# V with two keys per partition and copied-up odd keys, and expert weights as the moving operand in four column groups

## The chip, the core and the metric

The kernel runs on one core of one Trainium2 chip. The metric is device time in microseconds (us) of one execution. Several executions are made of each kernel, on the same chip as executions of the kernel before; medians are quoted with the lowest and highest run. A profiled execution gives the lines shown below. PE is the matrix engine (TensorE), PEld its weight loads, DVE is VectorE, ACT is ScalarE, POOL is GpSimd, SP is the engine that here only issues DMAs; a name with a q behind it (SPq, ACTq) is the engine's issuing of work. L243 is line 243 of that kernel. "Clock" is the mean share of full speed that was granted to PE.

Ratios are computed as the mean time of one kernel's fast runs over the mean time of the kernel before's fast runs in the same rounds, with a 95% interval. They are therefore not quite the ratio of the medians that are quoted. A run counts as fast when it is within 1.5% of the fastest run of its kernel, so a ratio can rest on few runs.

## The reference, cut to what matters

The computation is attention with "beacon" keys that every query may see, followed by a mixture of experts with soft slots.

```python
B, H, S, Nb, D = 8, 8, 576, 16, 64          # batches, heads, tokens, beacons, head size
k_all = concat([beacon_k, k], axis=2)       # 592 keys per head, beacons first
v_all = concat([beacon_v, v], axis=2)
scores = q @ k_all.T / sqrt(D)              # beacons always seen, the rest causal
a = exp(scores - max); a /= a.sum(-1)
x = (a @ v_all) -> reshaped to [4608, 512]

logits = x @ phi                            # [4608, 32]: 8 experts x 4 slots
slot_input = softmax(logits, axis=0).T @ x  # [32, 512]
for e in range(8):                          # w1 [512,1024], w2 [1024,512] per expert, float32
    slot_out[e] = relu(slot_input[e] @ w1[e]) @ w2[e]
out = softmax(logits, axis=1) @ slot_out    # [4608, 512]
```

## The kernel before

The loop goes over 32 pairs of heads, four pairs (g = 0 to 3) to a batch. In each step PE computes the scores of pair n in four pieces, ACT takes their exponential, POOL zeroes the entries above the diagonal, and PE multiplies the exponentials of pair n-1 with V. Work of the previous batch's routing is spread between. q and k are loaded five pairs ahead. V of the next batch is loaded in four parts, one per pair, and cast from float32 to float16 into `vh`, one key per partition.

```python
def load_v(b, part):
    for c in ((0, 1), (2,), (3,), (4,))[part]:          # c: block of 128 keys
        vf[(b, c)] = vfp.tile([P, H, D], FP, ...)
        if c == 0:
            nc.sync.dma_start(out=vf[(b, c)][0:Nb], in_=beacon_v[b].rearrange("h n d -> n h d"))
        lo, hi = max(0, c * P - Nb), min(S, (c + 1) * P - Nb)
        p0 = lo + Nb - c * P
        nc.sync.dma_start(out=vf[(b, c)][p0:p0 + hi - lo],
                          in_=v[b, :, lo:hi, :].rearrange("h p d -> p h d"))

def cast_v(b, c):
    (nc.vector if c % 2 else nc.gpsimd).tensor_copy(out=vh[b % 2][0:kn, c, :, 0:D], in_=vf[(b, c)][0:kn])

# in score(n, 0): one mask for the four diagonal blocks of both heads, on POOL
nc.gpsimd.affine_select(out=ex[n][:, :, 0:512]..., compare_op=AL.is_ge, fill=0.0, ...)

for n in range(NP + 1):
    ...                                                  # score, transp(n + 1), attend(n - 1)
    if n + 5 < NP:
        load_pair(n + 5)                                 # q and k
    if b + 1 < B:
        load_v(b + 1, g)
        for c in ((), (0, 1), (2,), (3, 4))[g]:
            cast_v(b + 1, c)
    if n % 3 != 2 and n >= 3 and wl < 24:
        load_w(wl); wl += 1                              # expert weights, 0.5 MB a piece, on POOL's queue

for e in range(E):                                       # experts: weights are the stationary operand
    for t in range(NFC):
        for c in range(NDC):
            nc.tensor.matmul(hp[:, t, :], w1h[e][:, c * F + t * P:c * F + (t + 1) * P],
                             siT[:, c, e * SPE:(e + 1) * SPE], ...)
    nc.scalar.activation(hTz[:, e, :, e * SPE:(e + 1) * SPE], hp[:, :, :], AF.Relu)
    for t in range(NFC):
        nc.tensor.matmul(sop[0:NSL, :], hTz[:, e, t, :], w2h[e][:, t * Dm:(t + 1) * Dm], ...)
```

The softmax here doesn't subtract the row's maximum and nothing guards it: scores larger than these inputs give would overflow.

## Time and profile before

The kernel before took 239.38 us (237.88 to 241.59, 3 runs); its profiled execution spans 239.4 us.

| what | before |
|---|---|
| attention with routing | to 181.5 us |
| experts | 181.5 to 211.2 us |
| output | 211.2 to 239.4 us |
| POOL idle until a V load landed | 28.5 us in 12 waits |
| steps of a batch that nothing disturbs | 3.45 + 3 x 4.76 = 17.7 us |
| steps of a batch as measured (starts of the key transposes) | 18.7 to 21.8 us |

The first fence is the view by windows of the kernel before: the window, its length, busy time of each engine with instruction counts, then the granted PE clock, the DMA engines' busy share and the GB/s moved.

```profile
core 0: us, PE busy (x) PEld busy (x) DVE busy (x) ACT busy (x) POOL busy (x), PEclk, DMA share, GB/s
0.00:24.00 24.00, 13.88 (x249) 10.61 (x249) 12.51 (x27) 9.83 (x11) 8.31 (x20) 1.00 1.05 249
24.00:181.50 157.50, 131.79 (x2911) 100.53 (x2910) 103.88 (x256) 104.16 (x150) 75.33 (x134) 0.92 0.99 220
181.50:211.20 29.70, 27.37 (x321) 13.70 (x321) 0.57 (x2) 1.58 (x8) 5.78 (x8) 0.77 1.06 186
211.20:239.40 28.20, 14.08 (x36) 4.25 (x35) 13.87 (x19) 11.83 (x18) 0.00 (x0) 0.58 0.81 335
```

The reader should see that in the attention no engine is busy for more than 84% of the window, while the DMA engines' share is 0.99. (The share is the sum of the packets' times over 16 engines, so it can exceed 1.)

The second fence is the view of POOL's waits, kernel before: what waited, for what, us in total, how often, the longest.

```profile
POOL vh_138 L243 <- DMA vf<-in_v_dram: 19.0, 7, 5.8
POOL vh_137 L243 <- DMA vf<-in_v_dram: 9.5, 5, 4.3
```

These two lines are the 28.5 us: POOL stands before a V cast because V has not landed, and the masks behind it in POOL's queue are late.

The third fence holds two of the costliest groups, kernel before (busy us, mean ns of one, then idle before it), and the fourth two DMA issues (KB each, median us from issue to landing).

```profile
L210 POOL TENSOR_SCALAR_AFFINE_SELECT ex<-ex 128x1024 f16<-128x1024 f16 x32 | 34.9, 1092 | 46.9 <-ACT ex L208 46.9
L243 POOL CAST vh_138<-vf 128x512 f16<-128x512 f32 (+1 forms) x12 | 7.7, 639 | 19.0 <-DMA vf<-in_v_dram 19.0
```

```profile
qf<-in_q_dram SPq DMA_DIRECT2D x32, 288.0 KB, 6.2
vf<-in_v_dram SPq DMA_DIRECT2D x24, 256.0 KB, 7.0
```

The trace also records every DMA packet with its size and duration. V moves in 37888 packets of 256 bytes, at 18 ns in the median (1024 packets of beacon keys have the same size and stay in all counts and sums for V here, 38912 packets in total); q and k in 8192 packets of 2304 bytes at 93 ns. The times of all packets of a kind, added up and divided by 16 engines, are called "packet time": V 54.0 us, q and k 56.0 us.

### The profile page before, as it was taken

How to read it: one execution, taken by the hardware profiler on the slowest of the kernel's cores; microseconds unless marked ns; L12 is line 12 of the kernel's file. 1: busy time of each engine (PE TensorE's matmuls, PEld its weight loads, DVE VectorE, ACT ScalarE, POOL GpSimd, SP SyncE). 2: the span in 40 equal slices, each digit the busy share in tenths (PEclk: the TensorE clock that was granted, in tenths of full speed). 3: DMA queues.
4: the chain of work that ended last, by engine and by line, in shares of the span. 5: the costliest groups of instructions: out<-in, count | busy, mean ns of one | idle time of the engine just before them, and what ended most of it. 6: DMA issues, size and time to landing. Idle time of an engine off the chain costs nothing.

```text
span 239.4 us, 8048 instructions
## 1 busy us (share of the span) xinstructions
PE 187.1 (78%) x3512; PEld 129.1 (54%) x3512; DVE 130.8 (55%) x304; ACT 127.4 (53%) x187; POOL 89.4 (37%) x161
## 2 busy tenths in 40 slices
PE   0579778869986898797898698899869999979800
PEld 0457566647664766575666476677646445532200
DVE  4583967555777566777667666566652000058800
ACT  2075576747767487776786758477710000057700
POOL 4080645442652732744645363443542420000000
PEclk9999889985999799999999979689996569995555
DMA  6999999999899899999999999272599999919995
GB/s 193 225 300 281 317 225 243 298 258 240 220 248 228 193 230 282 205 273 263 258 317 262 230 201 277 43 127 41 92 161 202 209 206 210 159 81 422 416 413 248
DMA packets 63715, 55.63 MB, mean 232 GB/s; under 512 B 41920, under 2 KB 50112, under 8 KB 62656
## 3 DMA queue, kind: packets, MB, share of 16 engines
q1 hardware_dynamic: 50880, 38.35, 56.3%
q0 software_dynamic: 12800, 16.78, 41.5%
q8 instruction: 27, 0.44, 0.8%
q14 instruction: 8, 0.07, 0.1%
HBM read 62.46 MB, written 9.44 MB: 300 GB/s over the span
## 4 chain that ended last, share of the span: by engine, by line
PE 47%; DMA 16%; ACT 13%; DVE 5%; SPq 5%; POOL 5%; issue 4%; ACTq 0%
DMA vf<-in_v_dram 14%; ACT ex L208 10%; PE av_152 L397 8%; PE sc_156 L202 6%; PE av_152 L229 6%; PE tr L187 6%; PE fp L413 5%; PE tr L256 3%; DVE xT L261 3%; PE tr L392 3%; PE sc_157 L202 3%; SPq L103 3%; PE tr L271 2%; PE av_153 L229 2%; DMA kf<-in_k_dram 2%
## 5 line engine op out<-in xcount | busy, mean ns | idle before, releaser
L208 ACT ACTIVATE ex<-sc_156 128x1024 f16<-128x1024 f32 x64 | 63.0, 984 | 47.4 <-PE sc_156 L202 47.2
L208 ACT ACTIVATE ex<-sc_157 128x992 f16<-128x992 f32 x64 | 48.0, 751 | 12.2 <-PE sc_157 L202 12.1
L210 POOL TENSOR_SCALAR_AFFINE_SELECT ex<-ex 128x1024 f16<-128x1024 f16 x32 | 34.9, 1092 | 46.9 <-ACT ex L208 46.9
L229 PEld LDWEIGHTS <-ex 128*128 128x128 f16 (+2 forms) x960 | 40.6, 113 | 12.8 <-issue 10.9
L397 PE MATMUL av_152<-w2h,hTz 128*32 128x512 f16 x64 | 20.1, 471 | 2.3 <-ACT hTz L395 2.3
L187 PE MATMUL tr<-idb,kf 64*64 64x64 bf16 x576 | 16.6, 204 | 2.0 <-issue 0.8
L261 DVE COPY xT<-tr 128x1024 f16<-128x1024 f16 x16 | 10.5, 687 | 13.2 <-PE tr L256 13.2
L187 PEld LDWEIGHTS <-qf 64*64 64x64 bf16 x576 | 13.4, 118 | 7.4 <-issue 6.2
L187 PE MATMUL tr<-idb,qf 64*64 64x64 bf16 x576 | 16.8, 205 | 0.6 <-DMA qf<-in_q_dram 0.5
L395 ACT ACTIVATE hTz<-tr 128x32 f16<-128x32 f32 x8 | 1.6, 198 | 28.8 <-PE tr L392 28.8
L401 DVE TENSOR_SCALAR soh<-av_152,rd 32x512 f16<-32x512 f32 x1 | 0.7, 737 | 29.0 <-PE av_152 L397 29.0
L187 PEld LDWEIGHTS <-kf 64*64 64x64 bf16 x576 | 14.3, 119 | 2.9 <-issue 2.6
L413 PE MATMUL fp<-soh,eLh 32*128 32x512 f16 x36 | 14.1, 522 | 1.4 <-DVE soh L401 0.8
L415 ACT ACTIVATE osb<-fp,rc 128x512 f32<-128x512 f32 x18 | 11.8, 687 | 5.9 <-PE fp L413 5.6
L202 PE MATMUL sc_156<-qT_129,kT_132 64*128 64x128 bf16 (+1 forms) x110 | 9.6, 276 | 6.9 <-POOL kT_132 L192 4.8
L243 POOL CAST vh_138<-vf 128x512 f16<-128x512 f32 (+1 forms) x12 | 7.7, 639 | 19.0 <-DMA vf<-in_v_dram 19.0
L216 POOL TENSOR_SCALAR_AFFINE_SELECT ex<-ex 80x160 f16<-80x160 f16 x32 | 10.6, 331 | 10.7 <-ACT ex L208 10.3
L202 PEld LDWEIGHTS <-kT_132 64*128 64x128 bf16 (+1 forms) x198 | 8.6, 110 | 11.1 <-POOL kT_132 L192 5.7
L417 DVE TENSOR_SCALAR osb<-fp,rc 128x512 f32<-128x512 f32 x18 | 13.1, 748 | 2.4 <-PE fp L413 1.6
L120 POOL DMA_DIRECT2D w1h<-in_moe_w_dram x16 | 11.5, 724 | 6.6 <-PE tr L392 6.6
L120 POOL DMA_DIRECT2D w2h<-in_moe_w_dram x16 | 12.1, 758 | 4.4 <-PE av_152 L397 4.4
L229 PE MATMUL av_153<-vh_138,ex 128*128 128x65 f16 (+2 forms) x240 | 11.5, 202 | 2.1 <-issue 2.1
(206 smaller groups left out, 318.9 us busy)
## 6 DMA issues: line engine op xcount, KB each, us to landing
qf<-in_q_dram SPq DMA_DIRECT2D x32, 288.0 KB, 6.2
kf<-in_k_dram SPq DMA_DIRECT2D x32, 288.0 KB, 6.3
w1h<-in_moe_w_dram POOLq DMA_DIRECT2D x16, 512.0 KB, 8.6
w2h<-in_moe_w_dram POOLq DMA_DIRECT2D x16, 512.0 KB, 8.9
out_dram<-osb SPq DMA_DIRECT2D x8, 1024.0 KB, 8.2
vf<-in_v_dram SPq DMA_DIRECT2D x24, 256.0 KB, 7.0
vf<-in_v_dram SPq DMA_DIRECT2D x8, 224.0 KB, 6.9
vf<-in_v_dram SPq DMA_DIRECT2D x8, 160.0 KB, 7.2
```

Source lines behind the costliest of these rows:

```text
L120: nc.gpsimd.dma_start(out=d[e][:, o:o + 2048].rearrange("p (c f) -> p c f", c=c), in_=src)
L187: nc.tensor.transpose(tp[po:po + 64, j, :], hi, idb[po:po + 64, po:po + 64])
L202: nc.tensor.matmul(sc[0:kn, a, col:col + un], kT[n % 3][64 * a:64 * a + 64, P * c:P * c + kn], qT[n % 3][64 * a:64 * a + 64, u0:u0 + un], ...
L208: nc.scalar.activation(ex[n][:, :, o:o + w], sc[:, :, 0:w], AF.Exp, scale=scale)
L210: nc.gpsimd.affine_select(out=ex[n][:, :, 0:512].rearrange("p a (c t) -> p a c t", c=4), in_=ex[n][:, :, 0:512].rearrange("p a (c t) -> p ...
L216: nc.gpsimd.affine_select(out=ex[n][0:UL, :, o:o + UL], in_=ex[n][0:UL, :, o:o + UL], compare_op=AL.is_ge, fill=0.0, base=0, pattern=[[0, ...
L229: nc.tensor.matmul(avs[a][0:m, i * DD:(i + 1) * DD], ex[n][0:kn, a, o:o + m], vh[b % 2][0:kn, c, h, :], start=(c == 0), stop=(c == i))
L261: nc.vector.tensor_copy(out=xT[b][:, :, P * cs[0]:P * cs[0] + 2 * P].rearrange("p t (i u) -> p i t u", i=2), in_=tp[:, :, :, :])
L397: nc.tensor.matmul(sop[0:NSL, :], hTz[:, e, t, :], w2h[e][:, t * Dm:(t + 1) * Dm], start=(e == 0 and t == 0), stop=(e == E - 1 and t == NF ...
L413: nc.tensor.matmul(fp_[:, :], etok(cg, j), soh[:, :], start=True, stop=True)
L415: nc.scalar.activation(osb[:, j, :], fp_[:, :], AF.Copy, scale=rc[:, i:i + 1])
L417: nc.vector.tensor_scalar(out=osb[:, j, :], in0=fp_[:, :], scalar1=rc[:, i:i + 1], scalar2=None, op0=AL.mult)
```

## The change

The intent is to move V in packets of twice the size and to shorten PE's work in the experts. A pair of neighbouring keys is put in one partition, so that a packet is 512 bytes. Blocks of scores below the diagonal then take even and odd keys separately, with rows chosen by a stride of 2. The blocks on the diagonal need keys in such an order that a 128-query block sees only 128 keys: for them a second copy `vn` is made, whose lower 64 partitions are the even keys and whose upper 64 the odd ones. POOL copies the even half, and a DMA from tile to tile (the "lift") moves the odd half up. The diagonal mask becomes a multiply on DVE with a fixed 0/1 tile; the triangular masks of the blocks beside the diagonal stay on POOL. In the experts the weights become the moving operand (512 columns), with the 32 slots as the stationary operand in four column groups.

```diff
 def load_v(b, part):
+    if part == 2:                                  # last 80 keys, one per partition, 256 B packets
+        nc.sync.dma_start(out=t[0:UL, :, :], in_=v[b, :, 4 * P - Nb:S, :].rearrange("h p d -> p h d"))
+    else:
+        t = vfp.tile([P, H, 2 * D], FP, name="vf", tag="vf")
+        vr = v[b].rearrange("h (r e) d -> r h (e d)", e=2)
+        if part == 0:
+            nc.sync.dma_start(out=t[0:Nb // 2, :, :], in_=beacon_v[b]...)          # partitions 0 to 7
+            nc.sync.dma_start(out=t[Nb // 2:P, :, :], in_=vr[0:P - Nb // 2, :, :]) # partitions 8 to 127
+        else:
+            nc.sync.dma_start(out=t[:, :, :], in_=vr[P - Nb // 2:2 * P - Nb // 2, :, :])
 ...
+        elif st == 3:                              # in score(): the blocks on the diagonal
+            z = ex[n][:, soff[3]:EW]
+            nc.vector.tensor_tensor(out=z, in0=z, in1=own..., op=AL.mult)
 ...
 def cast_v(b, part):
+    for e in range(2):
+        nc.gpsimd.tensor_copy(out=w[:, 2 * part + e, :, 0:D], in_=vf[(b, part)][:, :, e * D:(e + 1) * D])
+    nc.gpsimd.tensor_copy(out=vn[b % 2][0:64, part, :, :], in_=w[0:64, 2 * part, :, :])
+
+def lift_v(b):
+    for C in range(2):
+        nc.sync.dma_start(out=vn[b % 2][64:P, C, :, :], in_=vh[b % 2][0:64, 2 * C + 1, :, :])
 ...
             if b + 1 < B:
-                load_v(b + 1, g)
-                for c in ((), (0, 1), (2,), (3, 4))[g]:
-                    cast_v(b + 1, c)
+                for part in ((0, 1), (2,), (), ())[g]:
+                    load_v(b + 1, part)
+                if g > 0:
+                    cast_v(b + 1, g - 1)
+                if g == 2:
+                    lift_v(b + 1)
 ...
+def layer1(e):                                     # experts: weights move, 512 columns at a time
+    for f in range(2):
+        for c in range(NDC):
+            nc.tensor.matmul(sc[NSL * c:NSL * (c + 1), f, :], siT[:, c, :],
+                             w1h[e][:, c * F + f * 512:c * F + (f + 1) * 512], ...)
+    # copies to hs; turn(e) adds the four groups and transposes by a 0/1 "pick" matrix; layer2(e) alike
```

## The prediction

> What bounds the kernel now. The chain of waits has three stages: attention with routing until about 181 us, experts 181.5 to 211.2, output 211.2 to 239.4.
>
> Attention. Undisturbed, four pairs take about 17.7 us (3.45 + 3 x 4.75, starts of the key transposes in the timeline); measured batches take 19.3 to 21.8. The waits view names the cause: POOL sits 28.5 us before the V casts of line 243, waiting for V's loads; the masks and the kT copy queue behind, and PE stalls for 1.5 to 2.7 us (34.6, 75.9, 97.5, 135.7 us; also 25.3). Some of these stalls drop the granted clock to 0.5 (28, 79, 137 us). Together 12 to 13 us. A further 2.1 us gap at 50 us ("issue") with its slow clock is not V's. The DMA is also nearly full here (share 1.0 to 1.2 until 150 us): per batch, median packet times sum to about 19.2 us, of which V takes 5.3 (4736 packets of 256 B at 18 ns, 14 B/ns; the 2304 B packets of q and k reach 25 B/ns).
>
> Experts. PE is 90% busy, but the weight DMA runs without a gap from 174 to 209 us, 2.54 us per 0.5 MB piece; the last piece lands about 2 us before the experts end. So this stage is already almost DMA-bound.
>
> Output: DMA-bound at 420 GB/s.
>
> What the change does.
> 1. V goes in 512 B packets. [...] (18 ns at 256 B, 93 at 2304, 313 at 8192). My estimate is 28 to 31 ns at 512 B: V falls from 5.3 to about 4.3 us per batch, 8 us over the kernel.
> 2. V is loaded at least one pair before its cast; before, the last part was loaded and cast in the same pair. This should end POOL's V wait.
> 3. Masks: the 1092 ns one is gone; one of 512 and two of 256 columns come (estimated 630 and 405 ns from 290 ns at 128 and 1092 at 1024), plus a DVE multiply [...]. All casts move to POOL with two copies. POOL rises from 89 to about 120 us; in two of four pairs it does about 4.5 us of work in 4.75. That is thin.
> 4. Score and attention matmul counts (18 and 30 per pair) and exp widths (1680 per head) stay.
> 5. A lift DMA per batch, with slack of two pairs except at the start, where casts on POOL alone and the lift cost about 2 to 3 us.
> 6. Experts: per expert 64 column-streams of 128x128 weights become 16 of 512 columns in four column groups plus 8 small ones: about 4 us falls to about 2. But the DMA sets the pace, so only 1 to 3 us of up to 12 saved on PE appear.
>
> Sum: attention 12.5 less 2.5 = 10 earlier, weights' start moves along with it, experts 2.5, output 0: 239.4 - 12.5 = 226.9.
>
> Prediction: 227 us, range 219 to 235. Faster by over 2%: 0.82; within: 0.14; slower: 0.04.
>
> What would show it. POOL's wait for V under 5 us; batches near 18.5 us; fewer slow-clock stretches; weight DMA gapless, ending about 1 us before soh; PE in the expert stage with idle time "<-DMA w1h/w2h"; out stage still 28 us. V packets near 30 ns.
>
> What would make it wrong. POOL becomes the limit in the pairs with casts (kT and masks late): attention gains nothing. The lift blocks the load queue: it sits in order before q and k loads. Startup costs more than 3 us. Or column-tiled matmuls do not overlap: experts then gain nothing, though DMA hides most of this.

The sum came to 12.5 less 2.5 us in the attention and 2.5 us in the experts, 239.4 - 12.5 = 226.9. The 28 to 31 ns of step 1 are the author's estimate; a straight line through two of the medians beside it (18 ns at 256 bytes, 93 ns at 2304) gives 27.4 ns. The 2 to 3 us at the start (step 5) and the about 2 us per expert (step 6) are estimates too, for which the text gives no run.

## The result, and the profile after

The changed kernel is correct and slower: 251.12 us (247.83 to 251.55, 4 runs) against 239.63 us (237.88 to 241.59, 4 runs) for the kernel before; the ratio is 1.0545 (1.0437 to 1.0652). The profiled execution spans 249.3 us. Here is the view by windows, kernel after, cut at the same places of the program.

```profile
0.00:26.50 26.50, 12.10 (x204) 8.09 (x206) 11.79 (x30) 8.93 (x11) 11.93 (x35) 1.00 0.97 241
26.50:192.80 166.30, 138.95 (x2962) 105.41 (x2956) 118.55 (x272) 105.72 (x151) 103.66 (x222) 0.88 0.97 214
192.80:220.90 28.10, 17.43 (x195) 5.82 (x194) 6.11 (x10) 7.84 (x16) 5.77 (x8) 0.68 1.10 191
220.90:249.30 28.40, 11.92 (x38) 4.32 (x36) 13.47 (x19) 11.60 (x18) 0.00 (x0) 0.74 0.81 333
```

The experts fell from 29.7 to 28.1 us and the output stayed at 28 us. The whole loss is in the first two windows, 192.8 against 181.5 us. The DMA share did not fall there (0.97), although V's packets fell from 38912 to 22528.

The next fence is POOL's wait for V and SP's wait before the lift, kernel after, from the views of waits.

```profile
POOL vh L281 <- DMA vf<-in_v_dram: 6.6, 5, 2.9
SPq L287 <- POOL vh L281: 35.1, 13, 4.5
```

POOL's wait fell from 28.5 to 6.6 us, close to the "under 5" predicted, and the time did not follow. In its place SP, which issues all loads in order, stands 35.1 us before the lift, because the lift may go only when POOL has made the casts.

Most of the 6.6 us is two waits, of 2.91 and 2.58 us, and with them begin the two longest steps after the start, 8.56 and 8.22 us where 5.07 is undisturbed. This is the first of them (timeline, kernel after: start, length, what, and in brackets the idle time before it).

```profile
67.97 1.17 POOL L281 CAST vh<-vf 128x512 f16<-128x512 f32 x2 [2.91 <-DMA vf<-in_v_dram]
70.42 2.56 DVE L245 TENSOR_TENSOR ex<-ex,own 128x512 f16<-128x512 f16 x1 [0.27 <-ACT ex L226]
71.22 0.37 PE L207 MATMUL sc<-qT,kT 64*128 64x464 bf16 x2 [1.58 <-POOL kT L194]
73.31 0.72 PE L338 MATMUL tr<-dT,xb 128*128 128x32 f16 x20 [1.49 <-DVE dT L331]
```

POOL stands for V, then casts, copies, issues weights and masks before the small copy into `kT` that PE's next scores need; then a slow multiply on DVE holds up the copy `dT`. PE stands 1.58 and 1.49 us here, and 1.42 and 1.24 us in the other step. So POOL did become the limit in these two pairs.

The groups of the kernel after show three more places.

```profile
L265 PE MATMUL av<-vn,ex 128*128 128x65 f16 x128 | 24.9, 209 | 6.8 <-DMA vn<-vh 4.3
L245 DVE TENSOR_TENSOR ex<-ex,own 128x512 f16<-128x512 f16 x32 | 22.2, 695 | 7.3 <-ACT ex L226 6.0
L281 POOL CAST vh<-vf 128x512 f16<-128x512 f32 x32 | 19.1, 624 | 6.7 <-DMA vf<-in_v_dram 6.6
```

PE waits 4.3 us for a lift (once, at 17.6 us, in batch 0). The new multiply on DVE costs 695 ns in the mean; its median is 524 ns and its longest 2564. These are the DMA issues, kernel after.

```profile
qf<-in_q_dram SPq DMA_DIRECT2D x32, 288.0 KB, 10.8
vf<-in_v_dram SPq DMA_DIRECT2D x8, 512.0 KB, 9.7
vf<-in_v_dram SPq DMA_DIRECT2D x8, 480.0 KB, 11.2
vn<-vh SPq DMA_DIRECT2D x16, 65.0 KB, 3.9
```

q now lands 10.8 us after its issue instead of 6.2. The packet records say why V got no cheaper: the 16384 packets of 512 bytes took 41.2 ns in the mean and 40 in the median, not 28 to 31. V's packet time is 50.3 us, the lift adds 4.0 and q and k rose from 56.0 to 59.9, so that the three together went from 110.1 us to 114.2.

Batches took 22.5, 19.6, 23.6, 19.8, 19.7, 23.5 and 19.7 us. Steps that nothing disturbs take 3.55 + 4.78 + 5.08 + 5.07 us, so two steps of a batch are 0.3 us longer than before even then. The 11.3 us that the attention lost lie in three places: 3.9 us at the start (the second batch begins at 31.8 us, before at 27.9), 3.1 us in the next six batches (125.8 against 122.7 us), and 4.3 us in the last batch and the routing behind it (35.2 against 30.9 us; not taken apart).

### The profile page after: what moved, and what is told of

The parts are those of the page before. It is cut to its first block, busy times and chain, and to the rows that moved or that the text cites. A ratio compares the mean times of both kernels' runs of the same rounds, so it can differ in the third digit from the quotient of the medians.

```text
span 249.3 us, 7986 instructions
## 1 busy us (share of the span) xinstructions
PE 180.4 (72%) x3384; PEld 123.6 (50%) x3384; DVE 149.9 (60%) x331; ACT 134.1 (54%) x195; POOL 121.4 (49%) x264
## 5 line engine op out<-in xcount | busy, mean ns | idle before, releaser
L226 ACT ACTIVATE ex<-sc 128x928 f16<-128x928 f32 (+2 forms) x128 | 106.8, 868 | 64.4 <-PE sc L207 61.1
L229 POOL TENSOR_SCALAR_AFFINE_SELECT ex<-ex 128x256 f16<-128x256 f16 (+1 forms) x96 | 45.0, 483 | 58.2 <-ACT ex L226 43.7
L207 PE MATMUL sc<-qT,kT 64*64 64x128 bf16 (+3 forms) x576 | 51.1, 289 | 11.7 <-ACT ex L226 7.5
L265 PE MATMUL av<-vh,ex 128*128 128x65 f16 (+2 forms) x832 | 46.7, 210 | 0.9 <-issue 0.8
L191 DVE COPY qT<-tr 128x576 bf16<-128x576 bf16 x32 | 24.2, 756 | 18.8 <-PE tr L189 18.7
L207 PEld LDWEIGHTS <-kT 64*128 64x128 bf16 (+2 forms) x576 | 21.5, 108 | 24.7 <-issue 13.9
L271 DVE TENSOR_TENSOR xb<-av,r 128x320 f16<-128x320 f32 x64 | 31.5, 491 | 2.2
L265 PE MATMUL av<-vn,ex 128*128 128x65 f16 x128 | 24.9, 209 | 6.8 <-DMA vn<-vh 4.3
L245 DVE TENSOR_TENSOR ex<-ex,own 128x512 f16<-128x512 f16 x32 | 22.2, 695 | 7.3 <-ACT ex L226 6.0
L191 DVE COPY kT<-tr 128x576 bf16<-128x576 bf16 x32 | 23.9, 747 | 0.9 <-PE tr L189 0.8
L189 PE MATMUL tr<-idb,qf 64*64 64x64 bf16 x576 | 17.4, 209 | 1.3 <-DMA qf<-in_q_dram 0.5
## 6 DMA issues: line engine op xcount, KB each, us to landing
qf<-in_q_dram SPq DMA_DIRECT2D x32, 288.0 KB, 10.8
```

Source lines behind the costliest of these rows:

```text
L189: nc.tensor.transpose(tp[po:po + 64, j, :], hi, idb[po:po + 64, po:po + 64])
L191: nc.vector.tensor_copy(out=dst[:, Nb:Nb + S].rearrange("p (s j) -> p s j", j=J), in_=tp[:, :, :].rearrange("p j s -> p s j"))
L207: nc.tensor.matmul(sc[m0:m1, a, col:col + q1 - q0], kt[r, k0:k1:ks], qt[r, q0:q1], start=True, stop=True)
L226: nc.scalar.activation(x, sc[:, :, 0:w], AF.Exp, scale=scale)
L229: nc.gpsimd.affine_select(out=z, in_=z, compare_op=AL.is_ge, fill=0.0, base=P, pattern=pattern, channel_multiplier=-2)
L245: nc.vector.tensor_tensor(out=z, in0=z, in1=own[:, :, :].rearrange("p c t -> p (c t)"), op=AL.mult)
```

## The experiments

Two theories were set against each other at first. Theory W (the prediction's): V came late, and an earlier load cures the wait. Theory D: the attention is bound by DMA bandwidth, and V's wait is how that shows; a change that saves no packet time gains nothing, wherever the wait stands. On top of it come candidates for what the change itself costs: the lift in the load queue, the multiply ahead of other work on DVE, the start, and the price of the packets. "Before" is the kernel before.

### 1. Experts alone, attention alone

> Attention of the kernel before, logits on 128 rows, experts and output of the kernel after. If the whole loss lies in the attention part, this is 1 to 3 us faster than before (about 237), its expert stage ends within 2 us of the last weight piece, and PE idles there on w1h or w2h. Rival: the expert part costs time itself (128-row logits and exp, copies on ACT and DVE): then it is 2 us or more slower than before.

> Attention of the kernel after, experts of the kernel before. If the loss lies in attention: 251 to 254, 12 to 14 us slower than before. Rival (the expert part loses): near 240.

The first kernel is the kernel before with only the change's experts and router layout; the second is the change with the experts of before.

| kernel | median us | before | ratio (95%) |
|---|---|---|---|
| experts only (e1) | 239.23 (236.69 to 241.75) | 239.04 | 1.0078 (0.9973 to 1.0182) |
| attention only (e2) | 249.77 (247.41 to 250.85) | 239.04 | 1.0543 (1.0417 to 1.0669) |

The experts are neutral as far as the interval tells, and the attention carries the loss.

### 2. Is it when V comes, or how much comes?

```diff
-    vfp ... bufs=6            load_v(b + 1, g)
+    vfp ... bufs=8            load_v(b + 1, g + 1) for g < 3, load_v(b + 2, 0) for g == 3
```

> The kernel before, with every V load issued one pair earlier and 8 V buffers instead of 6; nothing else. Theory 'latency' (that of the prediction): POOL's wait for V falls from 28.5 us to under 5, its PE stalls go, 8 to 13 us faster than before (about 228). Rival 'DMA-bound': the engines are full in this stage, so an earlier issue moves the wait to the loads of q and k or elsewhere, and the time is within 1% of before.

The second kernel loads V of batch 0 only and uses it for all batches, so its result is wrong.

```diff
-                load_v(b + 1, g)
-        ... in_=vf[(b, c)][0:kn]
+        ... in_=vf[(0, c)][0:kn]
```

> Wrong result on purpose: the kernel before, with V of batch 0 loaded once and cast again for each batch, so 8.3 MB of V traffic are gone and POOL never waits for it. Theory 'DMA-bound attention': the loads then end some 40 us earlier, pairs fall to about 4.5 us, attention ends 12 to 18 us earlier and the time is 10 to 16 us under before. Rival 'PE and its slow clock bound it': under 4 us. Together with the run that loads V one pair earlier: if both gain the same, latency was the cause; if only this one gains, it was bandwidth.

| kernel (both on the kernel before) | median us | before | ratio (95%) |
|---|---|---|---|
| V one pair earlier, 8 buffers (e5) | 239.40 (237.72 to 239.95) | 238.45 | 1.0164 (1.0013 to 1.0314) |
| V of batch 0 only (e6) | 218.85 (216.65 to 219.63) | 238.45 | 0.9287 (0.9129 to 0.9446) |

POOL's wait with V one pair earlier, and the attention's first 160 us with V of batch 0 only (view of waits of the first, then view by windows of the second):

```profile
POOL vh L244 <- DMA vf<-in_v_dram: 21.6, 9, 4.8
```

```profile
0.00:160.00 160.00, 137.26 (x3190) 104.67 (x3191) 114.93 (x285) 113.53 (x162) 83.08 (x155) 1.00 0.87 203
```

The earlier load leaves 21.6 of the 28.5 us of waiting, and the time is no shorter (the medians differ by 0.4%). But this run is a weaker test than its name says. Counted from the start of the batch that uses it, a load of V was issued only about 1 us earlier in the mean than before, where a step is 4.8 us: SP's own issues of q, k and V took 97.9 us in sum, where they took 59.9 before (from 24 us on). The longest is this one (timeline of SP, V one pair earlier).

```profile
47.89 4.57 SPq L88 DMA_DIRECT2D qf<-in_q_dram  x1
```

Without V's traffic every batch after the first takes 17.7 us, exactly the four undisturbed steps, the clock stays at 1.00 and the DMA share falls to 0.87. But this run takes away V's wait and V's bytes at once. What tells the theories apart comes below: in the repaired kernel (section 4) POOL waits 2.1 us for V and the kernel is 3.4% slower than the one before; with cheaper packets and V's loads at the same places of the program (kernel a, section 5) it waits 1.3 us and the kernel is level. Ending V's wait did not bring the time, and fewer packet nanoseconds did. So theory W does not hold as the price of this stage. That V comes late because the DMA engines are full fits all these runs; no run shows it alone.

### 3. The lift in the load queue

Three edits of the change take the lift away from SP or leave it out.

```diff
 # lift one pair later, on ACT's queue
-                if g == 2: lift_v(b + 1)
+                if g == 3: lift_v(b + 1, nc.scalar)
 # no lift after batch 1 (wrong on purpose)
-                if g == 2: lift_v(b + 1)
+                if g == 2 and b == 0: lift_v(b + 1)
 # lift on ACT's queue, each half as soon as its cast is done, right after score(n, 0)
-                if g == 2: lift_v(b + 1)
+            if b + 1 < B and g > 1: lift_v(b + 1, (g - 2,), nc.scalar)
```

> The kernel after, with the steady-state lifts one pair later and on ACT's queue, so that the queue of q, k and V loads never waits for a cast. Theory 'blocked load queue': SP's wait for POOL falls from 35 us to about 5 (the start alone), V lands earlier, POOL's wait for V of 6.6 us goes, the two stalls of over 3 us at pairs 10 and 22 go: 6 to 10 us faster than after (about 243). Rival 'V's bytes and packets bound attention anyway' or 'DVE multiply': 0 to 2 us.

> Wrong result on purpose: the kernel after, with the lifts of batches 2 to 7 left out (the two that fill the buffers once stay). Theory 'blocked load queue': SP's wait for POOL goes from 35 to under 10 us and 4 us of lift packets go; 4 to 8 us faster than after. Rival 'the wait of the queue costs nothing because the engines have work queued': within 1% of after (251).

> The kernel after, right result, with each steady-state lift on ACT's queue and at least half a pair after its cast, but one pair earlier than in e3_lift_late, so that it neither blocks the queue of loads nor comes late. Theory 'the lift hurts by blocking the load queue': as the run without lifts (243), 6 to 9 us faster than after. Rival 'the lift's own packets, or the rest of the change, cost it': within 2 us of after (250).

| kernel (on the change) | median us | before | ratio (95%) |
|---|---|---|---|
| lift late, on ACT (e3) | 256.86 (253.64 to 257.91) | 239.04 | 1.0770 (1.0586 to 1.0954) |
| no lift (e7) | 242.64 (238.76 to 245.27) | 238.45 | 1.0214 (0.9801 to 1.0626) |
| lift early, on ACT (e9) | 250.86 (245.31 to 252.57) | 238.93 | 1.0404 (1.0261 to 1.0547) |

The first was a miss: the lift now landed too late, and PE stood before it (PE's waits, lift late; its profile was slow, so only the count of waits is used).

```profile
PE av L265 <- DMA vn<-vh: 9.6, 9, 3.6
```

The second has so wide an interval that it says little of the time; its profile, too, was slow. What it does show is that SP's wait before the lift is nearly gone; what remains is of the lifts of batches 0 and 1 (view of waits, no lift).

```profile
SPq L287 <- POOL vh L281: 5.3, 3, 2.9
```

In the third, SP's wait before the lift is down to 3.2 us (batch 0), and the kernel is still 4% slower than the kernel before. Its interval overlaps that of the change (1.0437 to 1.0652), so a gain from it is not proven. It also brought a wait of its own: the router's exponential stands in ACT's queue behind the lift, and PE waits for it (view of waits, lift early; the change has no such wait of PE).

```profile
PE tr L189 <- ACT eLh L319: 7.0, 6, 1.2
```

In six batches the third step now takes 6.35 us where it took 5.08 undisturbed; in return the two long steps are gone (the longest after the start is 7.07 us). So what SP's 35.1 us of waiting cost is not isolated by this run. The packets stayed at 41.2 ns.

### 4. The multiply on DVE, and the named costs together

The multiply is moved behind the routing pieces of the next step, so that copies PE waits for go first. The "repaired" kernel joins this to the early lift on ACT and gives half of batch 0's casts to DVE.

```diff
-        elif st == 3:                 # in score(n, 3)
-            nc.vector.tensor_tensor(out=z, in0=z, in1=own..., op=AL.mult)
+        if n >= 1: own_mask(n - 1)    # the same multiply, after score(n, 1)
 # repaired kernel, besides:
+            eng = nc.vector if b == 0 and e == 1 else nc.gpsimd    # in cast_v
```

> The kernel after, with the DVE multiply of the own blocks issued after the next pair's routing pieces instead of before. Theory 'multiply heads the DVE queue': the 0.8 us PE gap before the slot-input matmuls (8 of them in the trace of after) goes and undisturbed pairs with routing fall from 5.08 to about 4.75 us, in all 4 to 7 us faster than after (about 246). Rival 'load queue': under 2 us.

> e9 with two more repairs: the DVE multiply after the routing pieces (as e4), and at the start the odd keys of batch 0 cast by DVE and lifted first. The start stall of 4.3 us should fall to 1 to 2. If lift, start and multiply are the whole loss: 236 to 240, level with before. If it stays over 244, a cost is still unnamed.

| kernel (on the change) | median us | before | ratio (95%) |
|---|---|---|---|
| multiply later (e4) | 249.97 (246.50 to 251.21) | 239.04 | 1.0487 (1.0289 to 1.0684) |
| repaired (e10) | 244.96 (241.50 to 247.87) | 238.93 | 1.0339 (1.0247 to 1.0432) |

Moving the multiply brings the undisturbed step from 5.08 back to 4.76 us, yet the time stays, within the interval: POOL waits 8.6 us for V in this run, and two steps take 7.66 and 7.74 us. All repairs together take about 2% off the change. A loss of 3.4% stayed, with packets of 41.6 ns (view of waits, repaired).

```profile
POOL vh L283 <- DMA vf<-in_v_dram: 2.1, 3, 1.6
PE tr L189 <- ACT eLh L321: 4.3, 5, 1.1
```

V's wait is nearly gone. A part of the loss is again the lift on ACT: the third step of six batches takes 5.6 to 6.0 us where 4.76 is undisturbed, some 6 us in all. Kernel a) of the next section has the same wait (5.8 us) and is level. An estimate: without these 6 us and without PE's 3.7 us for batch 0's lift, the repaired kernel, which loses some 8 us, would be about level with the kernel before; ending V's wait was to make it 12 us faster.

### 5. The price of a 512-byte packet

The kernel before is given V in 512-byte packets, by two loads of 128 partitions that begin at partition 0, one pair apart; the beacons go to a tile that nobody reads. The data are in the wrong place; casts, masks and matmuls are untouched.

```diff
-        vf[(b, c)] = vfp.tile([P, H, D], ...)         # 256 B packets
+        t = vfp.tile([P, H, 2 * D], ...)
+        vr = v[b].rearrange("h (r e) d -> r h (e d)", e=2)
+        nc.sync.dma_start(out=t[:, :, :], in_=vr[64 * c:64 * c + P, :, :])   # c = 0, 2
```

> Wrong result on purpose (keys in another order): the kernel before with V in 512 B packets, two loads of 1/2 MB and a small one per batch, nothing else changed: no lift, no new masks. Theory 'a 512 B packet costs about 40 ns, so it carries no more than two of 256 B': V's packet time within 10% of before (54 us summed per engine) and the time within 1% of before. Theory of the prediction (28 to 31 ns): packet time under 42 us, and 5 to 8 us faster.

It (e12) took 230.80 us (229.94 to 231.61) against 238.93, ratio 0.974 (0.9661 to 0.982). The packets took 30.7 ns in the mean and 27 in the median. The DMA issues of that run:

```profile
qf<-in_q_dram SPq DMA_DIRECT2D x32, 288.0 KB, 5.4
vf<-in_v_dram SPq DMA_DIRECT2D x16, 512.0 KB, 7.4
```

So the prediction's price was attainable, and here it was worth 2.6% of the kernel, some 6 us, where the prediction's first step hoped for 8. Yet the change pays 40 ns for the same size. Two differences were left: the form of the first load (8 partitions of beacons, then 120 partitions that begin at partition 8), and the distance (the change issues both loads back to back). Four kernels set them apart, on one chip.

```diff
 # a) repaired kernel, both loads of 128 partitions from partition 0, beacons unused (wrong on purpose)
+            nc.sync.dma_start(out=t[:, :, :], in_=vr[P * part:P * part + P, :, :])
 # b) repaired kernel, the second load one pair later (right result)
-                for part in ((0, 1), (2,), (), ())[g]:
+                for part in ((0,), (1,), (2,), ())[g]:
 # c) repaired kernel, the first load as partitions 8 to 15 and 16 to 127 (right result)
+                for p0, p1 in ((Nb // 2, Nb), (Nb, P)):
+                    nc.sync.dma_start(out=t[p0:p1, :, :], in_=vr[p0 - Nb // 2:p1 - Nb // 2, :, :])
 # d) the cheap kernel above, with the change's form of the loads, one pair apart (wrong on purpose)
+            nc.sync.dma_start(out=t[0:Nb // 2, :, :], in_=beacon_v[b]...)
+            nc.sync.dma_start(out=t[Nb // 2:P, :, :], in_=vr[0:P - Nb // 2, :, :])
```

> The repaired kernel (lifts on ScalarE's queue, VectorE's multiply last, start casts on VectorE; 244.96 us, 512-byte packets 41.6 ns in the mean) with both V loads of 128 partitions, rows 0 to 127 and 128 to 255 of each head, issued back to back as before; the beacons go to unused partitions. The result is wrong on purpose. Theory A (the load of 120 partitions beginning at partition 8, next to one of 128, makes the packets dear): mean of the 512-byte packets 28 to 35 ns, time down by about 3 us or more. Rival B (two 512 KB loads back to back make them dear, whatever their partitions): 40 ns stays, and the time stays within 1%.

> The repaired kernel with the second V load of a batch issued one pair after the first, as in the kernel before; partitions as in the change; right result. Theory A (the form of the load): first load's packets stay dear, mean 36 to 42 ns, time within 1% of 245 us. Rival B (back to back): 28 to 32 ns, time down by about 3 us or more.

> The repaired kernel with the first V load split in two, partitions 8 to 15 and 16 to 127, so that the large one has 112 partitions[...]; right result. [...] If it is that the rows no longer begin at partition 0[...]: 40 ns stays.

> The kernel before with V in 512-byte packets (230.8 us, packets 30.7 ns), but with the change's own form of the loads: 8 partitions of beacons, 120 partitions from partition 8, then, a pair later, 128 partitions. Wrong result on purpose. Theory A (form of the load): packets rise to 36 to 42 ns, time rises by 2 us or more to 233 or above. Rival B (back to back only): packets stay at 29 to 32 ns and the time within 1% of 231.

| kernel | median us | before | ratio (95%) | 512 B packets, mean / median ns |
|---|---|---|---|---|
| a) from partition 0 (e13) | 237.30 (235.56 to 245.11) | 237.74 | 0.9997 (0.9921 to 1.0073) | 31.1 / 27 |
| b) one pair apart (e14) | 243.35 (241.68 to 246.80) | 237.74 | 1.0250 (1.0184 to 1.0316) | 36.3 / 28 |
| c) 8 + 112 partitions (e15) | 244.36 (240.55 to 252.13) | 237.74 | 1.0204 (1.0102 to 1.0306) | 38.8 / 38 |
| d) cheap kernel, change's form (e16) | 236.12 (234.04 to 236.77) | 237.74 | 0.9955 (0.9898 to 1.0012) | 37.5 / 33 |

Kernels a) and d) agree: the form of the first load makes the packets dear, and in the two kernels where it was tested it costs 2 to 3.5% of the kernel (the repaired kernel and a: 1.0339 and 0.9997; d and the cheap kernel: 0.9955 and 0.974; the intervals of each two are apart). Kernel b) shows it inside one run. In order of start, in groups of 256, the packets of its batch 7 took 30, 36, 47, 57 ns (the first load) and then 37, 30, 31, 38 ns (the second, of 128 partitions from partition 0); kernel a) has 27 to 33 ns all through that batch. Over all batches of b) the first load's packets took 39.9 ns in the mean and the second's 32.7. Distance alone, in b), recovers only the second load.

Is it the number of partitions, 120? Kernel c) was to test this, with a large load of 112. Its expectation had two alternatives. The first, packets below 36 ns and some 2 us less, was given a reason that no run shows. The second, that 40 ns stays, came nearest: 38.8 ns in the mean, 38 in the median. So 112 partitions in place of 120 did not make the packets cheap. What is left is the place of the rows in the partitions, or that there are fewer than 128 of them: no run has a large load of fewer than 128 partitions that begins at partition 0.

Why such a load makes packets dear is not shown; the trace names neither a packet's engine nor its place in the memory. What is shown is a median of 27 ns in the two kernels (e12 and a) where all large loads begin at partition 0, and of 28 to 40 ns, over the packets of both loads, where the first begins at partition 8 or 16.

### 6. With right data

The last two kernels try to get the cheap form with a right result. For batches 1 to 7 the first load covers all 128 partitions, with rows of the neighbouring head in the first 8; the beacons go to a tile of their own, and a POOL copy puts them over those 8 partitions. (The pool of tiles for the paired loads has 2 buffers in place of 3; in SP's view of waits V's loads wait 3.7 us for POOL in all, in the repaired kernel 5.3 and more.) The second kernel adds a direct load of batch 0's odd keys and later expert weights.

```diff
+                o = b * H * R - Nb // 2                    # 8 rows early; R = S // 2
+                nc.sync.dma_start(out=t[:, :, :], in_=v.rearrange("b h (r e) d -> (b h r) (e d)", e=2)
+                                  [o:o + H * R].rearrange("(h r) x -> r h x", r=R)[0:P])
 ...
+            nc.gpsimd.tensor_copy(out=w[0:Nb // 2, 0:2, :, 0:D], in_=vb.pop(b)[0:Nb // 2]...)  # before the vn copy
```

> A right-result form of the aligned loads in the repaired kernel: for batches 1 to 7 the first V load covers all 128 partitions, its first 8 partitions filled with rows that do not belong there; the beacons go to a tile of their own and one more copy on the Pool engine puts them over those 8 partitions. If it is the place of the rows in the partitions that made the packets dear: mean of the 512-byte packets 29 to 33 ns, time 236 to 240 us, level with the kernel before (ratio 0.99 to 1.01). If the aligned experiment gained for another reason (its wrong data, for instance): packets near 40 ns and 243 us or more.

> The kernel of e17 and two repairs more: the odd keys of batch 0 come straight from memory to the upper partitions, so that the first pair waits for no copy between tiles, and the expert weights that the attention has no time for are issued in its last pairs, three per pair, as in e11. Right result. Expected: the 3.6 us wait of PE for that copy at 16 to 18 us goes, the weights bring some 4 us as in e11; 228 to 234 us, ratio 0.96 to 0.985, level with e11 or better. If the loads of the last pairs collide with the weights, 234 us or more.

| kernel | median us | before | ratio (95%) | 512 B packets, mean / median ns |
|---|---|---|---|---|
| right data (e17) | 253.64 (251.69 to 258.50) | 239.50 | 1.0604 (1.0545 to 1.0664) | 33.7 / 31 |
| and all repairs (e18) | 258.92 (256.74 to 264.10) | 239.50 | 1.0841 (1.0768 to 1.0913) | 33.3 / 31 |

The packets answered nearly as expected, with right data, and the time missed by far. (The load of 8 partitions with the beacons is still there, so it is not what made the packets dear.) The cause is a new wait of the experiment's own making. First the timeline of POOL, right data, batch 3 (start, length, what; the profile was slow, but the same step of 7.40 us is in nearly every batch of both kernels, and the second kernel's profile was fast):

```profile
89.03 1.16 POOL L293 CAST vh<-vf 128x512 f16<-128x512 f32 x2
90.25 1.11 POOL L296 CAST vh<-vb 8x1024 f16<-8x1024 f32 x1
91.43 0.61 POOL L299 COPY vn<-vh 64x520 f16<-64x520 f16 x1
```

And the timeline of ACT in the same stretch.

```profile
91.39 0.47 ACTq L303 DMA_DIRECT2D vn<-vh  x1
91.91 0.41 ACT L335 ACTIVATE eLh<-tr 128x288 f16<-128x288 f32 x1 [2.50 <-DMA kf<-in_k_dram]
```

The copy of 8 partitions and 1024 columns takes 1.11 us, the two casts of 128 partitions and 512 columns before it 1.16 us together: here 8 partitions in place of 128 saved POOL next to nothing. The lift is issued from ACT, as in the repaired kernel, and has to wait for this copy too, and the router's exponential stands behind the lift in ACT's program: in this trace it starts at 91.91 us, after the lift's issue (91.39 us, 0.47 us long), and ACT has stood for 2.50 us. The trace names the load of k as the last to arrive; POOL's copy, which ends at 91.36, is what the lift at 91.39 was waiting for. PE waits with it. The view of waits of the second kernel has both:

```profile
PE tr L206 <- ACT eLh L342: 14.8, 6, 2.5
ACT eLh L342 <- POOL vh L303: 10.0, 4, 2.5
```

Six such waits of 2.5 us each, and a next step, with the second lift, that takes mostly 5.6 to 6.5 us instead of 4.8, make a batch of 22.2 us where 17.7 is the undisturbed one. In kernel a), without the copy, PE's wait at this place was 0.74 us in most batches. Whether the cheap packets with right data would bring the whole kernel level with the one before is therefore not shown: only with wrong data, in a). The difference between the two last kernels (1.0604 to 1.0841) was not taken apart.

### 7. Weights later

The attention of before leaves the DMA partly idle near its end. This is the line of the page that gives the GB/s in 40 equal slices of 6 us, kernel before:

```profile
GB/s 193 225 300 281 317 225 243 298 258 240 220 248 228 193 230 282 205 273 263 258 317 262 230 201 277 43 127 41 92 161 202 209 206 210 159 81 422 416 413 248
```

The four slices of 41 to 127 GB/s are 150 to 174 us, after the last q and k and before the last weights. Two kernels, both the kernel before with the change's experts, move weight pieces there.

```diff
-            if n % 3 != 2 and n >= 3 and wl < 24:
+            for _ in range(2 if n > 26 else int(n % 3 != 2 and n >= 3)):    # "fill"
+            for _ in range(3 if n > 26 else int(n % 2 == 0 and n >= 8)):    # "late"
```

> Attention of before and experts of after (as e1_experts_only), with two weight pieces per pair from pair 27 on, so that the 24 pieces that have buffers land while the engines are nearly idle (150 to 174 us) and only 8 are left for the expert stage. Theory 'weights set the pace of the expert stage': the last piece lands 5 to 8 us earlier and so does the end: about 233. Rival 'the expert stage has another limit' (its chain of copies, 2.3 to 2.7 us per expert): under 2 us.

> Attention of before, experts of after; 9 weight pieces before pair 27 instead of 16, then 3 per pair. Theory 'attention is bound by the DMA engines': with 24 us of weight traffic moved out of it, batches fall from 20.5 towards 18.5 us, the engines stay full from 140 us to the end of the experts: 224 to 232. Rival 'moving weights only moves the wait' : within 1% of e8_weights_fill (236).

| kernel | median us | before | ratio (95%) |
|---|---|---|---|
| fill (e8) | 235.95 (232.48 to 238.81) | 238.45 | 0.9937 (0.9726 to 1.0148) |
| late (e11) | 233.13 (232.68 to 242.44) | 238.93 | 0.9846 (0.9774 to 0.9918) |

The second is right and is the only version with a right result whose interval lies below the kernel before (it is faster by 1.5%); at the threshold of 2% the record calls it unclear. It fits section 2: weight pieces taken out of the crowded part of the attention are packet time that the attention does not have to share. Which of the two, the emptier attention or the fuller gap, brings the gain was not taken apart.

### Packet time and time, side by side

All numbers are of profiled runs; "sum" adds V, lift, q and k.

| kernel | V | lift | q and k | sum | ratio |
|---|---|---|---|---|---|
| before | 54.0 | 0 | 56.0 | 110.1 | 1 |
| V one pair earlier | 53.0 | 0 | 56.0 | 108.9 | 1.0164 |
| V of batch 0 only* | 7.9 | 0 | 53.8 | 61.6 | 0.9287 |
| 512 B from partition 0, kernel before* | 40.0 | 0 | 54.4 | 94.5 | 0.9740 |
| the same, change's form* | 46.4 | 0 | 56.1 | 102.4 | 0.9955 |
| the change | 50.3 | 4.0 | 59.9 | 114.2 | 1.0545 |
| repaired | 50.8 | 3.7 | 59.6 | 114.1 | 1.0339 |
| repaired, from partition 0* | 42.1 | 3.8 | 59.2 | 105.1 | 0.9997 |

(* wrong result.) Less packet time goes with less time, in the kernel before (V one pair earlier apart, whose ratio rests on two fast runs of the kernel before) and in the repaired change. But packet time is not the whole account: the change has only 4 us more of it than the kernel before and is 5% slower, and the repaired kernel, with the same sum as the change, 3%. What lies above is waits of its own. Of these the traces show PE's wait for batch 0's lift (4.3 us in the change, 3.6 in kernel a), the two long steps of the change (5.7 us of PE's waits), and the third steps with the lift on ACT (some 6 us in the repaired kernel). None was taken away alone. The granted clock moved too: until the experts it was 0.93 before, 0.90 in the change, 0.96 in the repaired kernel and 0.98 in kernel a). No run holds it fixed, so its part in these differences is not shown.

## Why the prediction was wrong

The prediction was 227 us (219 to 235) with 0.82 for faster; the result is 251.1 us, slower by 5%.

- **The step that failed is the main term: "Together 12 to 13 us"**, the gain from ending POOL's wait for V. The wait did shrink (28.5 to 6.6 us), and the six batches that should have gained took 125.8 us in place of 122.7. What failed is to take POOL's wait for V as the price of the stage: in the repaired kernel 2.1 us of it are left and the kernel is 3.4% slower than before, while cheaper packets (kernel a) make it level. V left out, wait and bytes together, gained 7%. The prediction wrote itself that "the DMA is also nearly full here" and then costed the stage by POOL's wait. Here the wait for V behaved like a symptom: as it shrank, q's landing grew (6.2 to 10.8 us).
- **Step 1, V's packets, was mis-sized in this change.** 28 to 31 ns were predicted; loads from partition 0 take 27 ns in the median, but the change's take 40. (The straight line that gives 27.4 ns at 512 bytes gives 309 at 8192, where 313 were measured; what it leaves out is the form of the load.) In the repaired kernel they fall from 40 to 27 when its first load, 120 partitions from partition 8, is made 128 from partition 0. Packet time for V with its lift is 54.3 us, against 54.0 before: nothing saved instead of 8 us. The form of the load alone costs 2 to 3.5% in the two kernels where it was tested, the largest single part of the loss that was isolated.
- **Step 2 was nearly right as a statement about the wait** (6.6 us, under 5 predicted) and step 3 about POOL: 121.4 us busy, 120 predicted. The masks came out at 637 ns (512 columns) and 406 ns (256 columns), 630 and 405 predicted. The risk that was named with it, POOL as the limit in pairs with casts, came true in the two steps of 8.56 and 8.22 us.
- **The multiply was mis-sized**: it takes 695 ns in the mean, and the prediction's figure, which came from no run, was too small. In the two longest (2.4 and 2.56 us) POOL worked without a pause throughout; that POOL is the cause is not shown, since no run takes its work away. The multiply also stands ahead of copies PE waits for, 0.3 us in two steps of a batch; moving it did not change the time measurably.
- **Step 5, the lift**: its possible harm in the load queue was named as a risk, and SP did stand 35.1 us there. Taking the lift out of that queue moved the ratio from 1.0545 to 1.0404, with overlapping intervals, and put 7.0 us of PE's waits behind ACT. The start cost 4.3 us of PE's time, predicted 2 to 3.
- **Step 6, experts, was nearly right**: 1 to 3 us predicted, 1.6 us in the profile's window, and by time no gain that the interval can tell from zero (1.0078, 0.9973 to 1.0182). PE's own work did shrink: from the start of the first to the end of the last, the eight matmuls of an expert's second layer take 1.07 us where they took 3.59 (timelines of PE, both at a granted clock of 0.50; 0.61 and 1.90 at 1.00). The reason given, that DMA sets the pace there, fits: after the change PE is busy 17.4 of 28.1 us, the stage is hardly shorter, and the last weights land at 220.2 us, 0.7 us before its end.
- **What stays open**: how the loss divides among packet time, the start, the two long steps, the longer multiply steps and the clock; the 4.3 us in the last batch and behind it; whether the place or the number of the partitions makes packets dear, and why; and what cheap packets with right data would give without the new wait.

## What to carry to other kernels

When a stage's DMA engines are busy all the time (a share of 0.97 to 0.99 in the attention here), cost a change there by packet time, packets times their measured nanoseconds, and take a wait for a load only as a sign of it; leaving the load out (with a wrong result) tells in one run what its wait and its bytes are worth together. When a load is moved earlier in the program, check in the trace how much earlier it was issued. Check the price of a packet in the form in which the change will use it: the size alone does not set it, and with a first load of 120 partitions from partition 8 a packet took 40 ns where it took 27 with loads of 128 partitions. The lift issued from ACT put its wait into ACT's order of work: where it had to wait for POOL's extra copy, ACT stood 2.50 us in a step (right data), and PE 14.8 us in six waits (all repairs). So what a DMA on a computing engine waits for should be finished well before.
